# TensorE instead of DMAs spreads the fourth head pair in steps 0 to 3 of a linear-attention and feed-forward kernel

## The chip, the cores and the metric

The kernel runs on one core of one Trainium2 chip. The metric is the device time of one execution, in microseconds (us).

## The reference

Two stages. The first is a recurrent attention over 768 tokens, for 4 sequences and 8 heads of 48 channels; the second a feed-forward block over all 3072 tokens (384 channels, 2048 hidden), with no expert routing in it.

```python
for t in range(S):                       # r, k, v: (4, 8, 768, 48); w, u: (8, 48)
    cur   = u * k_t (outer) v_t
    y[t]  = r_t @ (state + cur)
    state = w * state + k_t (outer) v_t
x = y.transpose(0, 2, 1, 3).reshape(3072, 384)
h = x @ w_in
g = h * tanh(log1p(exp(h)))
out = g @ w_out
```

## The kernel before

**Attention.** The 768 tokens are cut into 6 chunks of 128 tokens; with 4 sequences this makes 24 steps, s = 4 * chunk + sequence. A step holds r and k of its chunk transposed (tile `rk`; for steps 2 and 3 `rkx`), k in natural layout (`kn`, later `rkn`) and v (`v`, for steps 2 and 3 `vx`). VectorE scales r and k by powers of w (L381). In steps 0 to 3 the diagonal terms come from a product `q` (L392, VectorE), eight columns by TensorE (`sd`, L399) and a copy (L402, ScalarE); ScalarE then writes the diagonal matrices of the 8 heads into `P` (L426). TensorE forms the scores `pa` (L456), VectorE puts those below the diagonal into `P` under a mask (L463, one instruction for each of two halves), and TensorE multiplies `P` by v into `yt` (L487). From step 4 on the product with the running state `S` is added (L495). `st` (L524) is the outer product of k and v that advances the state; for it VectorE first multiplies k by a table (`kn<-kn,TKn`, L440).

**Rows of x.** The feed-forward contracts over 384 channels in 3 blocks of 128 rows. Heads go in pairs; a pair fills rows 0 to 47 and 64 to 111 of a block. Rows 48 to 63 and 112 to 127 of the three blocks take the fourth pair, 16 channels each. In `finish`, ScalarE copies the fourth pair from `yt` to a side tile `st` (L568), then the first three pairs to `x` (L573), and six DMAs on SyncE's queue move the side tile's rows to their places in `x` (L585). In steps 0 to 3 these six DMAs come for every step, later for every two steps. Event `x{s}` says that x of step s is complete.

**Feed-forward.** Tokens of one chunk of all four sequences make a group g (512 columns). A group has 16 up tiles n (128 hidden channels each, tile `hp`, then copied to `hb` at L748) and 16 down tiles (`acc`). Between them ScalarE runs sigmoid, arctangent and sine with two table loads (L643 to L649) and VectorE a product (L654 in group 0). In group 0 the matmuls are fp32 (L632 up, L676 down); from group 1 on three fp32r products take their place (L610). The first four up tiles of group 0 are cut into pieces of one sequence, 3 matmuls each (L707, 16 pieces), so that they can start when `x0` is complete. Up tile 4 is the first whole one. Down tile n - 6 follows up tile n.

**Weights.** 16 chunks of 768 KB are loaded by GpSimd's queue (`wraw`, L268), 8 for `w_in` and 8 for `w_out`, and converted from 64-bit to 32-bit floats by ScalarE (L286, L292) and VectorE (L288 to L298; the last of a conversion is L298). I write U0, U1, ... for the chunks of `w_in` (two up tiles each) and D0, D1, ... for those of `w_out`. Later each chunk is split into two fp32r halves (L311 ScalarE, L313 VectorE).

**Order.** The kernel writes out the order of every engine's instructions itself. Small generators (threads) yield an engine and a cost or the name of an event; a planner (`Flow`) picks the thread that can go first, ties by rank. A planned wait of TensorE longer than `WARM_MIN` is filled with dummy matmuls (`idle`, L229) by `flow.fill`, until the first piece of L707 is issued. The lead constants shift ranks, in up tiles: `L_IN` and `L_OUT` for the conversions and splits of `w_in` and `w_out`, `L_ATT` for the attention steps. On the chip each engine runs its list in order and waits at each instruction for what it needs; so an instruction that waits holds up all that stand behind it on that engine. SyncE's queue holds the loads of `rk`, `kn`, `rkn`, `v` and the DMAs of L585.

Of the kernel before, what the change touches and what calls it, by code (L numbers as in the profile page):

```python
# [10 lines left out]
F32 = mybir.dt.float32  # L11
F32R = mybir.dt.float32r
# [5 lines left out]
ALU = mybir.AluOpType  # L18
# [3 lines left out]
B, H, S, D = 4, 8, 768, 48  # L22
NP = H // 2
C = 128
NC = S // C
NS = NC * B
DM, DFF = H * D, 2048
KT = DM // 128
# [12 lines left out]
HALVES = (slice(0, 64), slice(64, 128))  # L41
# [9 lines left out]
LAG = 6  # L51
LO0, HI0, LO1, HI1 = 0.10, 0.92, 0.05, 0.85
LAT, LAT0 = 0.15, 0.13
WARM0, WARM_MIN, FILL = 32, 0.3, 1.1
DMA_LAT = 2.0

COST = dict(dve=1.5)
FREE = dict(pe=8.0, act=4.5, dve=2.0, pool=1.7, sp=1.0)

L_ATT, L_V, L_IN, L_OUT, L_GATE, L_EVAC, L_PUT, L_FIN = 4, -2, 2, 4, 2, 12, 9, 4  # L60


class Flow:
# [60 lines left out]
def dve(cols, fast=False):  # L124
    return {"dve": 0.14 + cols / (1900 if fast else 950)}


def act(cols):
    return {"act": 0.1 + cols / 1060}


def pe(us):
    return {"pe": us}
# [3 lines left out]
def rwkv_mish_kernel(ctx, tc, rkT, rkN, vN, wT, w_in, w_out, consts, rkF, vF, wF, uF, outT):  # L137
    nc = tc.nc
# [4 lines left out]
    work = main.enter_context(tc.tile_pool(name="work", bufs=2))  # L143
# [10 lines left out]
    us = cst[:, 256 : 256 + 2 * NP].rearrange("d (p q) -> d p q", q=2)  # L154
# [15 lines left out]
    loaded = {}  # L170
# [10 lines left out]
    def prologue():  # L181
# [16 lines left out]
        nc.vector.tensor_copy(TRK[:, 1], TR[:, :, ::-1])  # L198
        flow.set("TRK")

    def token_table():
        dw = work.tile([128, NP, 2, D], F32, name="dw", tag="fa", bufs=1)
        yield {"pool": 1.5}
        nc.gpsimd.memset(dw, 0.0)
        yield "TRK"
        for par in range(2):
            r = ROWS[par]
            yield dve(192)
            nc.vector.tensor_tensor(
                out=dw[r, :, par], in0=ident[r, r].unsqueeze(1).broadcast_to([D, NP, D]),  # L210
                in1=w128[r].unsqueeze(2).broadcast_to([D, NP, D]), op=ALU.mult,
            )
        yield pe(1.0)
        t = ps.tile([128, 512], F32, name="tkn", tag="acc1")
        for p in range(NP):
            nc.tensor.matmul(
                t[:, 2 * p * D : 2 * (p + 1) * D], lhsT=TRK[:112, 1, p, :],
                rhs=dw[:112, p].rearrange("d q e -> d (q e)"), start=True, stop=True,
            )
        yield act(384)  # L220
        nc.scalar.copy(out=TKn, in_=t[:, :DM])
        flow.set("TKn")
# [3 lines left out]
    def keep_warm(n):  # L226

        for _ in range(n):
            nc.tensor.matmul(idle[:, :256], lhsT=zeros, rhs=zeros.unsqueeze(1).broadcast_to([128, 2, 128]), start=True, stop=True)  # L229
# [3 lines left out]
    flow = Flow(FREE)  # L233
    flow.events["wt"] = 3.5
    for c in range(2 * NW):
        flow.events[f"raw{c}"] = 8.5 + 4.0 * min(c, 3) + 2.3 * max(c - 3, 0)
    flow.fill = lambda us: keep_warm(int(us * FILL / 0.112))
    ok = const.tile([32, 1], I32, name="ok")

    def check_range():  # L240
# [77 lines left out]
    xs, sides = {}, [None]  # L318
# [3 lines left out]
    def load_early():  # L322

        both = work.tile([128, 2, 2, NP, C], F32, name="rkx", tag="x")
        vx = work.tile([128, 2, 2, NP, 64], F32, name="vx", tag="gh")
        for s in range(B):
            if s < 2:
                rk = stage.tile([128, 2, NP, C], F32, name="rk", tag="rk")
                v = stage.tile([128, 2, NP, 64], F32, name="v", tag="v")
            else:  # L330
                rk, v = both[:, s - 2], vx[:, s - 2]
            if s % 2 == 0:
                kn = stage.tile([128, 2, DM], F32, name="kn", tag="rkn")
            loaded[s] = rk, kn[:, s % 2], v
            yield {"sp": 2.4}
            nc.sync.dma_start(rk[:112], rkT[s])
            flow.set(f"rk{s}")
            yield {"sp": 1.4}
            nc.sync.dma_start(v, vN[s])
            flow.set(f"v{s}")  # L340
        yield "x0"
        for s in range(B):
            yield {"sp": 0.55}
            nc.sync.dma_start(loaded[s][1], rkN[s][:, 1])
            flow.set(f"rkn{s}")

# [122 lines left out]
    def outputs(s):  # L469
        c, b = divmod(s, B)  # L470
        last = c == NC - 1
        yield f"masked{s}"
        yield f"v{s}"
        if c:
            yield f"state{s - B}"
            if not last:
                yield f"keys{s}"
        if s:
            yield f"y{s - 1}"
        yield from paced(s, 1)  # L480
        yield pe(1.05 * (1 + (c > 0)) + (0.6 if 0 < c < NC - 1 else 0))
        rk, n, v = loaded[s][:3]
        P = Ps.pop(s)
        y = ps.tile([128, 512], F32, name="yt", tag="yt")
        for p in range(NP):
            for par in range(2):
                nc.tensor.matmul(  # L487
                    y[HALVES[par], p * C : (p + 1) * C], lhsT=v[:, par, p, :], rhs=P[:, p, par, :],
                    start=not c or p == 0, stop=not c,
                )  # L490
        if c:
            for p in range(NP):
                for par in range(2):
                    r = ROWS[par]
                    nc.tensor.matmul(  # L495
                        y[r, p * C : (p + 1) * C], lhsT=Sc[b][r, p, :], rhs=rk[r, 0, p, :], start=False, stop=p == NP - 1
                    )
        flow.set(f"out{s}")
        flow.start(finish(s, y), rank(s) - L_FIN)
        if not c:  # L500
            flow.start(first_state(s), s - 899.5)
        elif not last:
            st = state_products(s, "pa0")
            r = slice(0, 112)
            yield dve(192)
            nc.vector.tensor_tensor(
                out=Sc[b][r], in0=Sc[b][r], in1=w128[r].unsqueeze(2).broadcast_to([112, NP, D]), op=ALU.mult
            )
            for par in range(2):
                r = ROWS[par]  # L510
                yield dve(192)
                nc.vector.tensor_tensor(
                    out=Sc[b][r], in0=Sc[b][r], in1=st[r, : NP * D].rearrange("d (p e) -> d p e", p=NP), op=ALU.add
                )
        if c:
            flow.set(f"state{s}")
# [28 lines left out]
    def finish(s, y):  # L545
        g, b = divmod(s, B)
        if b == 0:
            if g >= 2:
                yield f"ups{g - 2}"
            if g:  # L550
                xs[g] = work.tile([128, KT, B, 2, C], F32R, name="x", tag="x")
            else:
                xs[g] = work.tile([128, KT, B, 1, C], F32, name="x0", tag="x")
        x = xs[g]
        y = y.rearrange("m (k t) -> m k t", k=NP)
        if g:
            if b % 2 == 0:
                yield f"x{s - 1}"
                sides[0] = work.tile([128, 2, 2, C], F32R, name="st3", tag="st3", bufs=1)
            side = sides[0][:, b % 2]  # L560
        else:
            if b % 2 == 0 and b:
                yield f"x{s - 1}"
            if b % 2 == 0:
                sides[0] = work.tile([128, 2, 1, C], F32, name="st0", tag="st3", bufs=1)
            side = sides[0][:, b % 2]
        yield act(128)
        nc.scalar.copy(out=side[:, 0], in_=y[:, 3])  # L568
        if g:
            yield dve(128)  # L570
            nc.vector.tensor_tensor(out=side[:, 1], in0=y[:, 3], in1=side[:, 0].bitcast(F32), op=ALU.subtract)
        yield act(384)
        nc.scalar.copy(out=x[:, :, b, 0], in_=y[:, :3])  # L573
        if g:
            yield dve(384)
            nc.vector.tensor_tensor(out=x[:, :, b, 1], in0=y[:, :3], in1=x[:, :, b, 0].bitcast(F32), op=ALU.subtract)
        flow.set(f"y{s}")
        if g and b % 2 == 0:
            return
        n = 2 if g else 1  # L580
        yield {"sp": 0.6}
        for k in range(KT):
            for par in range(2):
                o = 64 * par
                nc.sync.dma_start(  # L585
                    x[o + D : o + 64, k, b + 1 - n : b + 1].bitcast(F32).rearrange("e b a t -> e (b a t)"),
                    sides[0][o + 16 * k : o + 16 * k + 16, b % 2 + 1 - n : b % 2 + 1].bitcast(F32).rearrange("e b a t -> e (b a t)"),
                )
        if n == 2:
            flow.set(f"x{s - 1}")  # L590
        flow.set(f"x{s}")

    def place(s, piece):
# [239 lines left out]
    for c in range(len(W_ORDER)):  # L833
        i, f = W_ORDER[c]
# [12 lines left out]
    with tc.If(in_range < 128 * NP):  # L847
# [3 lines left out]
        with tc.tile_pool(name="any1", bufs=1) as work:  # L851
# [22 lines left out]
            with tc.For_i(0, S, TB) as t0:  # L874
# [6 lines left out]
                for t in range(TB):  # L881
# [7 lines left out]
                    for hf in range(2):  # L889
                        y = ps.tile([128, 512], F32, name="hp", tag="hp", bufs=2)  # L890
# [5 lines left out]
        with tc.tile_pool(name="any2", bufs=1) as work:  # L896
            xt = work.tile([128, KT, 2, 64], F32, name="xt")
            x = work.tile([128, KT, 1, 2, C], F32R, name="x")
            for b in range(B):
                with tc.For_i(0, S, 128) as t0:  # L900
# [4 lines left out]
                    t = ps.tile([128, 512], F32, name="t", tag="yt")  # L905
# [4 lines left out]
                    t = t[:, : KT * 128].rearrange("m (k t) -> m k t", k=KT)  # L910
# [79 lines left out]
```

## Time and profile before

| | us |
|---|---|
| median of 3 runs | 568.77 (568.34 to 572.46) |
| the profiled execution | 566.41 |
| its span, first to last instruction | 563.8 |
| TensorE busy (dummy matmuls included) | 535.8 |
| VectorE busy | 372.9 |
| ScalarE busy | 401.7 |
| granted TensorE clock, mean | 0.96 |

The profile is of one execution. Busy times are sums over the span. A row of the timeline gives start, duration, engine, line, operation, tiles, count, and in square brackets how long the engine had stood idle before it and what ended that. The profile counts two matmuls and two weight loads for one fp32 matmul of the program.

### The profile page before, as it was taken

The numbers are of one execution on the slowest core, as the hardware profiler recorded it, in microseconds if no ns is written. First come the engines' busy times: TensorE is split into PE (matmuls) and PEld (weight loads), VectorE is DVE, ScalarE is ACT, GpSimd is POOL, SyncE is SP. The second block draws the span as 40 slices with busy tenths as digits, with TensorE's granted clock in tenths as the row PEclk, the third lists the DMA queues.
The fourth block names the chain that finished last, engine by engine and source line by source line (L and its number), as shares of the span: only waits on it lengthen the run. The fifth ranks groups of instructions, "written<-read, shape, count | busy, mean of one in ns | idle before, by whom it ended". The sixth has DMA issues, their size and how long they took to land. (4 is left out here: it accounts for less than half of the span.)

```text
span 563.8 us, 8124 instructions
## 1 busy us (share of the span) xinstructions
PE 535.8 (95%) x3223; PEld 406.5 (72%) x3223; DVE 372.9 (66%) x560; ACT 401.7 (71%) x479; POOL 10.6 (2%) x26
## 2 busy tenths in 40 slices
PE   6996986999999999999999999999999999999995
PEld 5875743454566787877878887788887778888884
DVE  5554798799677788557587667685666664455552
ACT  2642699577788778887866867865958785859770
POOL 4110000000000000000000000000000000000000
PEclk8758888899999999999999999999999999999998
DMA  8993522120302430302422122322024000010001
GB/s 286 352 405 148 163 68 73 34 80 1 94 1 80 132 98 9 86 5 94 131 80 65 29 59 67 104 80 77 18 80 128 24 0 16 0 51 6 1 0 60
DMA packets 17902, 46.36 MB, mean 82 GB/s; under 512 B 3200, under 2 KB 4096, under 8 KB 17856
## 3 DMA queue, kind: packets, MB, share of 16 engines
q1 hardware_dynamic: 12816, 28.13, 17.2%
q0 software_dynamic: 2304, 12.58, 5.9%
q10 hardware_dynamic: 2736, 5.05, 2.5%
q8 instruction: 27, 0.44, 0.3%
q14 instruction: 19, 0.16, 0.1%
HBM read 38.87 MB, written 4.72 MB: 77 GB/s over the span
## 5 line engine op out<-in xcount | busy, mean ns | idle before, releaser
L610 PE MATMUL hp<-x,w 128*128 128x512 f32 x720 | 182.3, 397 | 0.0
L610 PE MATMUL acc<-gh,w 128*128 128x512 f32 x480 | 159.8, 389 | 0.0
L610 PEld LDWEIGHTS hp<-x,w 128*128 128x128 f32 x720 | 132.7, 188 | 31.6 <-issue 2.6
L610 PEld LDWEIGHTS acc<-gh,w 128*128 128x128 f32 x480 | 90.1, 188 | 18.8
L610 PE MATMUL acc<-gl,w 128*128 128x512 f32 x240 | 93.4, 389 | 0.0
L643 ACT ACT_TABLE_LOAD x48 | 61.6, 1283 | 15.8 <-DVE gf L654 8.0
L748 DVE COPY hb<-hp 128x512 f32<-128x512 f32 x49 | 33.8, 690 | 52.2 <-PE hp L610 46.0
L643 ACT ACTIVATE fa<-hb,bias_ln 128x1024 f32<-128x1024 f32 x48 | 55.3, 1151 | 13.2 <-DVE hb L656 12.7
L656 DVE TENSOR_TENSOR hb<-hb,fa 128x1024 f32<-128x1024 f32 x40 | 48.8, 1220 | 21.4 <-ACT fa L649 21.4
L649 ACT ACT_TABLE_LOAD x48 | 61.6, 1283 | 0.9
L610 PEld LDWEIGHTS acc<-gl,w 128*128 128x128 f32 x240 | 45.0, 188 | 9.4
L646 ACT ACTIVATE fa<-fa 128x1024 f32<-128x1024 f32 x48 | 50.9, 1060 | 1.1
L649 ACT ACTIVATE fa<-fa 128x1024 f32<-128x1024 f32 x48 | 50.9, 1060 | 0.5
L664 DVE TENSOR_TENSOR gl<-hb,gh 128x1024 fp32r<-128x1024 f32 x40 | 48.8, 1220 | 2.1 <-ACT gh L660 1.8
L463 DVE COPY_PREDICATED P<-cst,pa 128x512 f32<-128x512 uint32 x48 | 34.4, 730 | 17.5 <-PE pa L456 17.4
L748 ACT COPY hb<-hp 128x512 f32<-128x512 f32 x47 | 27.5, 585 | 25.3 <-PE hp L610 16.5
L676 PE MATMUL acc<-gf,wraw 128*128 128x512 f32 x96 | 44.6, 600 | 0.0
L632 PE MATMUL hp<-x,wraw 128*128 128x512 f32 x72 | 35.5, 633 | 6.8 <-DVE wraw L298 6.8
L381 DVE TENSOR_TENSOR rk<-rk,TRK 112x512 f32<-112x512 f32 x44 | 29.7, 684 | 5.2 <-DMA rk<-in_rkT_dram 5.2
L676 PEld LDWEIGHTS acc<-gf,wraw 128*128 128x128 f32 x96 | 18.8, 198 | 19.7 <-issue 19.0
L660 ACT CAST gh<-hb 128x1024 fp32r<-128x1024 f32 x16 | 16.8, 1052 | 21.0 <-DVE hb L656 13.2
L632 PEld LDWEIGHTS hp<-x,wraw 128*128 128x128 f32 x72 | 14.3, 207 | 22.1 <-issue 14.6
(86 smaller groups left out, 540.3 us busy)
## 6 DMA issues: line engine op xcount, KB each, us to landing
rk<-in_rkT_dram SPq DMA_DIRECT2D x22, 448.0 KB, 4.2
rkn<-in_rkN_dram SPq DMA_DIRECT2D x20, 384.0 KB, 4.3
wraw<-in_w_in_dram POOLq DMA_DIRECT2D x8, 768.0 KB, 19.2
wraw<-in_w_out_dram POOLq DMA_DIRECT2D x8, 768.0 KB, 19.6
v<-in_vN_dram SPq DMA_DIRECT2D x22, 256.0 KB, 4.3
out_dram<-ob ACTq DMA_DIRECT2D x18, 256.0 KB, 2.0
x<-st SPq DMA_DIRECT2D x60, 32.0 KB, 2.0
rkx<-in_rkT_dram SPq DMA_DIRECT2D x2, 448.0 KB, 18.4
```

Of the source, the lines that this page charges most:

```text
L381: nc.vector.tensor_tensor(out=rk[:112, a], in0=rk[:112, a], in1=TRK[:112, a], op=ALU.mult)
L463: nc.vector.copy_predicated(out=Ps[s][:, :, par], mask=mask.unsqueeze(1).broadcast_to([128, NP, C]), data=pa[par].rearrange("j (p i) -> j ...
L610: nc.tensor.matmul(out, lhsT=a, rhs=m, start=first and n == 0, stop=last and n == 2)
L632: nc.tensor.matmul(hp[:, :T], lhsT=e[:, fs], rhs=o.x[:, k, :, 0], start=k == 0, stop=k == KT - 1)
L643: nc.scalar.activation(o.g, o.hb, AF.Sigmoid, bias=bias_ln2, scale=1.0)
L646: nc.scalar.activation(o.g, o.g, AF.Arctan)
L649: nc.scalar.activation(o.g, o.g, AF.Sin, scale=2.0)
L656: nc.vector.tensor_tensor(out=o.hb, in0=o.hb, in1=o.g, op=ALU.mult)
L660: (nc.scalar.copy if engine == "act" else nc.vector.tensor_copy)(out=o.gh, in_=o.hb)
L664: nc.vector.tensor_tensor(out=o.gl, in0=o.hb, in1=o.gh.bitcast(F32), op=ALU.subtract)
L676: nc.tensor.matmul(a, lhsT=whole[1, f // WG][:, ws], rhs=o.gf[:, j], start=f == 0, stop=f == NF - 1)
L748: (nc.scalar.copy if engine == "act" else nc.vector.tensor_copy)(out=o.hb[:, j], in_=h)
```

## The change

For steps 0 to 3 `finish` no longer copies the fourth pair to a side tile and issues no DMA. Instead ScalarE copies the fourth pair's v, 16 channels for each of three blocks, to the last 16 of 64 columns of a zeroed tile (`pre` for even steps, `pre2` for odd ones; 48 columns stay zero), and TensorE adds a second product to each block of `yt` in the same accumulation: `P` of the fourth pair by that tile. So `yt` has the rows of `x` in their places, 6 matmuls by v and 6 by the spread tile where there were 8, and one ScalarE copy writes `x`. GpSimd zeroes both tiles ahead of its first weight load. The loads of `kn` for steps 0 to 3 no longer wait in the planner for `x0`. Dummy matmuls: 28 at the start for 32; later gaps filled from 0.5 us on, with at most 16. `L_IN` 2 to 6, `L_OUT` 4 to 8, `L_ATT` 4 to 3.

```diff
-WARM0, WARM_MIN, FILL = 32, 0.3, 1.1
+WARM0, WARM_MIN, FILL = 28, 0.5, 0.7
-L_ATT, L_V, L_IN, L_OUT, L_GATE, L_EVAC, L_PUT, L_FIN = 4, -2, 2, 4, 2, 12, 9, 4
+L_ATT, L_V, L_IN, L_OUT, L_GATE, L_EVAC, L_PUT, L_FIN = 3, -2, 6, 8, 2, 12, 9, 4
...
+    pre = work.tile([128, 2, 2, KT, 64], F32, name="pre", tag="fa", bufs=1)
+    pre2 = work.tile([128, 2, KT, 64], F32, name="pre2", tag="st3", bufs=1)
+    nc.gpsimd.memset(pre, 0.0)
+    nc.gpsimd.memset(pre2, 0.0)
+    dw = pre[:, 0].rearrange("d a b c -> d (a b c)").rearrange("d (p q e) -> d p q e", p=NP, q=2)
+    spread = (pre[:, 1], pre2)
...
-    flow.fill = lambda us: keep_warm(int(us * FILL / 0.112))
+    flow.fill = lambda us: keep_warm(min(16, int(us * FILL / 0.15)))
...
-        yield "x0"
         for s in range(B):
-            yield {"sp": 0.55}
+            yield {"sp": 1.0}
             nc.sync.dma_start(loaded[s][1], rkN[s][:, 1])
...
+        else:
+            if s >= 2:
+                yield f"out{s - 2}"
+            engine = yield {**act(96), "dve": 0.25}
+            v = loaded[s][2]
+            (nc.scalar.copy if engine == "act" else nc.vector.tensor_copy)(
+                out=spread[s % 2][:, :, :, D:], in_=v[:, :, KT, :D].rearrange("t q (k e) -> t q k e", k=KT)
+            )
...
-        for p in range(NP):
+        for p in range(NP if c else KT):
             for par in range(2):
-                nc.tensor.matmul(
-                    y[HALVES[par], p * C : (p + 1) * C], lhsT=v[:, par, p, :], rhs=P[:, p, par, :],
-                    start=not c or p == 0, stop=not c,
-                )
+                out = y[HALVES[par], p * C : (p + 1) * C]
+                nc.tensor.matmul(out, lhsT=v[:, par, p, :], rhs=P[:, p, par, :], start=not c or p == 0, stop=False)
+                if not c:
+                    nc.tensor.matmul(
+                        out, lhsT=spread[s % 2][:, par, p, :], rhs=P[:, KT, par, :], start=False, stop=True
+                    )
...
+        if not g:
+            yield act(384)
+            nc.scalar.copy(out=x[:, :, b, 0], in_=y[:, :KT])
+            flow.set(f"y{s}")
+            flow.set(f"x{s}")
+            return
...
-        yield {"sp": 0.6}
+        yield {"sp": 3.6}
```

How the order moves, at three places. On SyncE's queue, after the loads of `rk` and `v` of steps 0 to 3, before the change:

```order
L339 DMA vx<-in_vN_dram 128x512
L585 DMA x_305<-st_306 16x128 x6
L344 DMA kn<-in_rkN_dram 128x384 x4
L585 DMA x_305<-st_306 16x128 x6
L585 DMA x_305<-st_448 16x128 x12
L352 DMA rk<-in_rkT_dram 112x1024
```

and with it (the load of `vx` is the same instruction, four lines further down in the file):

```order
L343 DMA vx<-in_vN_dram 128x512
L347 DMA kn<-in_rkN_dram 128x384 x4
L355 DMA rk<-in_rkT_dram 112x1024
L360 DMA rkn<-in_rkN_dram 128x768
L355 DMA rk<-in_rkT_dram 112x1024
```

All 24 small DMAs are gone, and the loads of `kn` and of steps 4 and 5 stand directly behind `vx`.

On TensorE, around `y` of step 1 and the first piece of an up tile (`hp<-x`), before:

```order
L229 MATMUL idle<-zeros 128x256
L399 MATMUL sd<-cst,q 128x2 x4
L487 MATMUL yt<-P,v 64x128 x8
L707 MATMUL hp<-x_305,wraw 128x128 x3
L456 MATMUL pa_393<-rkx 128x128
```

and with the change (`pre` is the spread tile of step 0, `pre_98` that of step 1, whose matmuls go on behind the last row):

```order
L501 MATMUL yt<-P,pre 64x128
L402 MATMUL sd<-cst,q 128x2 x4
L715 MATMUL hp<-x_310,wraw 128x128 x3
L499 MATMUL yt<-P,v 64x128
L501 MATMUL yt<-P,pre_98 64x128
```

The first piece stands ahead of `y` of step 1 instead of behind it, and the dummies between are gone.

On VectorE, around the two masks of step 3 (`pa_453` and `pa_454` before, `pa_427` and `pa_428` with the change), where `kn<-kn,TKn` waits for the loads of `kn`, `we` and `wraw` are conversions of weights, and L313 or L317 a split. Before:

```order
L440 TENSOR_TENSOR kn<-kn,TKn 128x384 x4
L294 TENSOR_SCALAR we<-we 128x768
L463 COPY_PREDICATED P<-cst,pa_453 128x4x128
L296 SCALAR_TENSOR_TENSOR we<-wraw,we 128x768
L463 COPY_PREDICATED P<-cst,pa_454 128x4x128
L298 ISA wraw<-wraw,we 128x768x2
L290 TENSOR_SCALAR we<-we 128x768
L313 TENSOR_TENSOR w<-wraw,w 128x768
```

and with the change:

```order
L443 TENSOR_TENSOR kn<-kn,TKn 128x384 x2
L294 TENSOR_SCALAR we<-we 128x768 x2
L466 COPY_PREDICATED P<-cst,pa_427 128x4x128
L298 TENSOR_SCALAR we<-we 128x768
L466 COPY_PREDICATED P<-cst,pa_428 128x4x128
L300 SCALAR_TENSOR_TENSOR we<-wraw,we 128x768
L298 TENSOR_SCALAR we<-we 128x768
L302 ISA wraw<-wraw,we 128x768x2
L300 SCALAR_TENSOR_TENSOR we<-wraw,we 128x768
L317 TENSOR_TENSOR w<-wraw,w 128x768
L294 TENSOR_SCALAR we<-we 128x768
L302 ISA wraw<-wraw,we 128x768x2
```

The masks still stand behind all waits for `kn`. Chunks U2 and U3 are now converted side by side right there, and further on, between the end of D0's conversion and the end of U7's, VectorE's list has 98 instructions where it had 109.

More of the change, by code (lines that the diff above doesn't have):

```diff
@@ L199, in prologue @@
         flow.set("TRK")
+    pre = work.tile([128, 2, 2, KT, 64], F32, name="pre", tag="fa", bufs=1)
[4 more added lines that the diff above has]
+    spread = (pre[:, 1], pre2)
     def token_table():
-        dw = work.tile([128, NP, 2, D], F32, name="dw", tag="fa", bufs=1)
-        yield {"pool": 1.5}
-        nc.gpsimd.memset(dw, 0.0)
         yield "TRK"
@@ L473, in outputs @@
         yield f"v{s}"
+        if s:
+            yield f"y{s - 1}"
         if c:
@@ L477, in outputs @@
                 yield f"keys{s}"
-        if s:
-            yield f"y{s - 1}"
+        else:
[6 more added lines that the diff above has]
+            )
         yield from paced(s, 1)
-        yield pe(1.05 * (1 + (c > 0)) + (0.6 if 0 < c < NC - 1 else 0))
+        yield pe(1.05 * (1 + (c > 0)) + (0.6 if 0 < c < NC - 1 else 0) if c else 1.5)
         rk, n, v = loaded[s][:3]
@@ L555, in finish @@
         y = y.rearrange("m (k t) -> m k t", k=NP)
[L556 to L566, printed above, removed]
+        if not g:
[4 more added lines that the diff above has]
+            return
+        if b % 2 == 0:
+            yield f"x{s - 1}"
+            sides[0] = work.tile([128, 2, 2, C], F32R, name="st3", tag="st3", bufs=1)
+        side = sides[0][:, b % 2]
         yield act(128)
         nc.scalar.copy(out=side[:, 0], in_=y[:, 3])
-        if g:
-            yield dve(128)
-            nc.vector.tensor_tensor(out=side[:, 1], in0=y[:, 3], in1=side[:, 0].bitcast(F32), op=ALU.subtract)
+        yield dve(128)
+        nc.vector.tensor_tensor(out=side[:, 1], in0=y[:, 3], in1=side[:, 0].bitcast(F32), op=ALU.subtract)
         yield act(384)
         nc.scalar.copy(out=x[:, :, b, 0], in_=y[:, :3])
-        if g:
-            yield dve(384)
-            nc.vector.tensor_tensor(out=x[:, :, b, 1], in0=y[:, :3], in1=x[:, :, b, 0].bitcast(F32), op=ALU.subtract)
+        yield dve(384)
+        nc.vector.tensor_tensor(out=x[:, :, b, 1], in0=y[:, :3], in1=x[:, :, b, 0].bitcast(F32), op=ALU.subtract)
         flow.set(f"y{s}")
-        if g and b % 2 == 0:
+        if b % 2 == 0:
             return
-        n = 2 if g else 1
-        yield {"sp": 0.6}
+        yield {"sp": 3.6}
         for k in range(KT):
@@ L585, in finish @@
                 nc.sync.dma_start(
-                    x[o + D : o + 64, k, b + 1 - n : b + 1].bitcast(F32).rearrange("e b a t -> e (b a t)"),
-                    sides[0][o + 16 * k : o + 16 * k + 16, b % 2 + 1 - n : b % 2 + 1].bitcast(F32).rearrange("e b a t -> e (b a t)"),
-                )
-        if n == 2:
-            flow.set(f"x{s - 1}")
+                    x[o + D : o + 64, k, b - 1 : b + 1].bitcast(F32).rearrange("e b a t -> e (b a t)"),
+                    sides[0][o + 16 * k : o + 16 * k + 16].bitcast(F32).rearrange("e b a t -> e (b a t)"),
+                )
+        flow.set(f"x{s - 1}")
         flow.set(f"x{s}")
```

## The prediction

> **What bounds the kernel now.** The page's busy shares and its slices come first.
>
> ```profile
> span 563.8 us, 8124 instructions
> PE 535.8 (95%) x3223; PEld 406.5 (72%) x3223; DVE 372.9 (66%) x560; ACT 401.7 (71%) x479; POOL 10.6 (2%) x26
> PE   6996986999999999999999999999999999999995
> ```
>
> TensorE is the bound on average, but its row has holes in the first seven slices of 14.1 us only. So I split the span with the windows view (core, then busy time and count of PE, PEld, DVE, ACT and POOL, granted clock, DMA share, GB/s).
>
> ```profile
> 26.00:66.00 40.00, 31.71 (x249) 27.34 (x250) 22.16 (x36) 15.18 (x37) 2.22 (x5) 0.74 0.67 253
> 66.00:141.10 75.10, 66.66 (x366) 34.92 (x366) 66.66 (x113) 60.74 (x85) 0.00 (x0) 0.93 0.21 59
> 141.10:557.00 415.90, 415.90 (x2465) 327.09 (x2460) 270.95 (x378) 312.94 (x329) 0.00 (x0) 1.00 0.18 55
> ```
>
> From 141.1 us to 557.0 TensorE is never idle, at full clock, with the other engines at 65% to 75%. Its work there does not change. So the question is **how much earlier TensorE reaches the point that is at 141.1 now**, the start of up tile 14. Ahead of it lie a head (to 65.85, the first whole up tile) and a middle. The timeline of TensorE shows where each loses time.
>
> ```profile
> 45.79 0.47 PE L707 MATMUL hp<-x,wraw 128*128 128x128 f32 x2 [2.88 <-DMA x<-st]
> 56.19 2.39 PE L707 MATMUL hp<-x,wraw 128*128 128x128 f32 x18
> 65.85 2.85 PE L632 MATMUL hp<-x,wraw 128*128 128x512 f32 x6
> 98.29 4.88 PE L632 MATMUL hp<-x,wraw 128*128 128x512 f32 x6 [4.99 <-DVE wraw L298]
> 128.09 2.85 PE L632 MATMUL hp<-x,wraw 128*128 128x512 f32 x6 [1.77 <-DVE wraw L298]
> 141.12 2.85 PE L632 MATMUL hp<-x,wraw 128*128 128x512 f32 x6
> ```
>
> In the head it waits for rows of x that DMAs bring; in the middle for conversions (L298), and after the long wait of 4.99 us its first tile takes 4.88 us instead of 2.85.
>
> **The head, removed.** Who waits for the small DMAs, in the timelines of ScalarE and SyncE's queue:
>
> ```profile
> 47.75 0.27 ACT L568 COPY st<-yt 128x128 f32<-128x128 f32 x1 [12.17 <-DMA x<-st]
> 47.91 0.49 ACT L573 COPY x<-yt 128x384 f32<-128x384 f32 x1
> 29.01 2.19 SPq L344 DMA_DIRECT2D kn<-in_rkN_dram x4
> 32.88 27.16 SPq L585 DMA_DIRECT2D x<-st  x18
> ```
>
> The side tile has one buffer, so step 2's copy waited 12.17 us until step 1's six DMAs had landed, behind four loads of `kn`. `y` of step 3 could follow only then, and 18 DMAs kept the queue to 60 us. All of that goes. What is late next? VectorE's list:
>
> ```profile
> 25.99 0.69 DVE L392 TENSOR_TENSOR q<-rkx 112x512 f32<-112x512 f32 x1 [5.91 <-PE idle L229]
> 44.69 0.56 DVE L440 TENSOR_TENSOR kn<-kn,TKn 128x384 f32<-128x384 f32 x1 [3.36 <-DMA kn<-in_rkN_dram]
> 47.11 0.72 DVE L463 COPY_PREDICATED P<-cst,pa 128x512 f32<-128x512 uint32 x1
> 57.55 0.96 DVE L296 SCALAR_TENSOR_TENSOR we<-wraw,we 128x768 uint32<-128x768 uint32 x1
> 58.42 0.55 DVE L294 TENSOR_SCALAR we<-we 128x768 uint32<-128x768 uint32 x1
> 58.89 0.95 DVE L298 CUSTOM_DVE_ANT_0 wraw<-wraw,we 128x1536 uint16<-128x1536 uint16 x1
> ```
>
> The `q` at 25.99 is that of step 3. The dummies named had ended before, so it waited for its load of `rkx`, which the change leaves where it is; shorter filling ahead of this point gains nothing, since the masks of step 1 stand behind that `q`. The second bound is the last `kn`: the masks of step 3 stand behind it in both lists, and it came at 44.69. With the change its load follows `vx` on the queue:
>
> ```profile
> 5.46 0.59 SPq L339 DMA_DIRECT2D vx<-in_vN_dram  x1
> DMA to landing us min/median/max: 19.0/21.0/23.0
> DMA to landing us min/median/max: 6.9/9.6/13.8
> ```
>
> The second row is `vx`, the third `kn`. The last `vx` lands at 5.46 + 23.0 = 28.5. Behind it the four `kn`, 768 KB, come at the latest after what they needed before, 44.7 - 29.0 = 15.7 us: 44.2, hardly a gain. At the earliest they come soon after 28.5, but TensorE's own list is the next bound then, priced by these rows:
>
> ```profile
> 24.69 1.05 PE L399 MATMUL sd<-cst,q 112*128 112x2 f32 x8
> 53.77 1.09 PE L487 MATMUL yt<-P,vx 128*64 128x128 f32 x16
> 58.50 0.56 PE L524 MATMUL st<-vx,kn 128*48 128x48 f32 x16
> 36.36 4.21 PE L707 MATMUL hp<-x,wraw 128*128 128x128 f32 x18
> 125.16 1.16 PE L456 MATMUL pa<-rk 48*128 48x128 f32 x16
> 28.00:42.00 14.00, 12.64 (x77) 0.54 1.03 405
> ```
>
> Steps 0 to 3 have 12 matmuls for 8, so 24 records for 16: a `y` takes 1.09 x 24/16 = 1.64 us, 0.55 more than before. A piece has 6 records at 2.39/18 = 0.133: 0.8. Step 1's masks end at 25.99 + 2.4 = 28.4. From there to `y` of step 3 TensorE's list holds two `y`, one `sd`, two scores, six pieces and two `st`: 3.3 + 1.05 + 2.3 + 4.8 + 1.1 = 12.5 us, to 40.9 at full clock. At the 0.54 of the window from 28 to 42 it would be 23.1 us, to 51.5. So the masks of step 3 bind if `kn` comes after 37.7. I take **41.0** for `kn`, the middle of 37.7 and 44.2. From there the `kn` instruction, three conversions and two masks, with spacings of 0.47 and 0.61 us, end 3.2 us later, as the chain from 44.69 to 47.83 did: 44.2, which a clock at half for the first 7 of those us (28.4 + 7 + 9 = 44.4) would give as well.
>
> Then `y` of step 3 ends at 45.8, and ScalarE's one copy adds 0.7 (0.49 and the handover). Nine pieces stand behind it in the new order: 7.2. Two `st` add 1.1. **The first whole up tile starts at 54.8** instead of 65.85. The ends are 51.5 (`y` of step 3 at 40.9) and 62.1 (at 51.5); with `kn` at 44.2 alone it is 58.0.
>
> Those ends hang on the clock, which shorter filling could lower:
>
> ```profile
> 42.00:48.00 6.00, 2.19 (x22) 0.99 0.89 348
> 48.00:51.00 3.00, 3.00 (x27) 0.50 0.08 27
> ```
>
> A third of 6 us busy, and the clock falls to half only behind it, though the next 3 us are full of work. [...]
>
> [...]
>
> **The middle.** TensorE's own work from up tile 4 to up tile 14, by the spacings of these rows:
>
> ```profile
> 112.13 1.09 PE L487 MATMUL yt<-P,v 128*64 128x128 f32 x16
> 114.66 2.85 PE L632 MATMUL hp<-x,wraw 128*128 128x512 f32 x6
> 117.34 2.74 PE L676 MATMUL acc<-gf,wraw 128*128 128x512 f32 x6
> 119.92 2.74 PE L632 MATMUL hp<-x,wraw 128*128 128x512 f32 x6
> ```
>
> 10 up and 8 down tiles at 2.62 (2.68 and 2.58 from row to row), four times scores (1.09) and `y`, `S` and `st` together (114.66 - 112.13 = 2.53): 47.2 + 4.4 + 10.1 = 61.7 us. It took 141.1 - 65.85 = 75.3, so 13.6 are lost. With nothing lost tile 14 would start at 54.8 + 61.7 = 116.5. But it needs chunk U7, and VectorE converts. Its list has 109 instructions from the end of D0's conversion to the end of U7's; the window counts one more at its edge.
>
> ```profile
> 65.13 0.95 DVE L298 CUSTOM_DVE_ANT_0 wraw<-wraw,we 128x1536 uint16<-128x1536 uint16 x1
> 66.08:138.65 72.57, 64.15 (x110) 0.93 0.21 61
> 137.74 0.94 DVE L298 CUSTOM_DVE_ANT_0 wraw<-wraw,we 128x1536 uint16<-128x1536 uint16 x1
> ```
>
> VectorE was 88% busy there, and a step of its list took 72.57/110 = 0.66 us, waits in. With the leads raised the same stretch has 98 instructions, since splits and later steps fall behind it: 64.7 us. It begins at the end of D0's conversion. Behind the masks (44.2) stand 14 instructions up to it, by the spacings of the three conversions quoted eight of 0.87 and five of 0.47, and a copy of 0.3, 9.6 us, and a wait that I put at 1.4, since the second split among them needs room that tile 1's last piece frees: 55.2. So U7 is ready at **55.2 + 64.7 = 119.9**, 3.4 us after TensorE could take it. I add 0.6 for matmuls at a low clock behind such waits: tile 14 at 120.5, **20.6 us earlier**. Behind it the list holds the splits that were pushed back. Group 1, with three products for one, leaves more time for each chunk, so I take no more than another 0.6 us off.
>
> ```profile
> 66.08:138.65 72.57, 58.62 (x82) 0.93 0.21 61
> 2.23 0.42 POOL L204 MEMSET dw<- 128x384 f32 x1
> ```
>
> ScalarE (first row) works 58.6 of those 72.6 us, so it is less tight. GpSimd zeroes three times the columns of the second row, 1.3 us, ahead of the first weight load; the load at 25.99 hides that, and without this cover the head would be later by as much. Each spread copy is a ScalarE instruction of 96 columns, a quarter of the 0.49 us copy and a fixed part, while ScalarE waits 12.17 us in one place there.
>
> **The sum.** The profiled execution took 566.4 us (span 563.8 and 2.6 around it), below the three timed runs, whose median is 568.77. 20.6 - 0.6 = 20.0: 546.4 for the profile, and **548.8** against the median.
>
> **The rivals.**
> (a) TensorE never waits in the middle: 116.5, or 113.2 with the early head, so 24.6 to 27.9 us earlier: 541 to 544. For it: 98 instructions at 64.15/110 = 0.58 are 57.2 us, and 55.2 + 57.2 = 112.4. Against it: VectorE would have to have no wait at all. 15%.
> (b) Only the head is gained and the middle loses its 13.6 us again, since conversions, masks and copies share one list: 11.0 us, 557.8; with the late `kn` 7.9 us, 560.9. For it: VectorE is 88% busy. Against it: 11 instructions fewer ahead of U7. 25%.
> (c) Slower: each conversion now stands ahead of something that TensorE waits for. VectorE's list is in order, so a mask or copy of `hp` in the middle can stand behind one whole conversion, 0.87 + 0.87 + 0.47 + 0.47 = 2.7 us. With 4 steps and 10 up tiles waiting so, 38 us come on top of 20.0 gained: 587. It decides from 20.0/14 = 1.4 us each. Against it: of the 13.6 us lost in the middle now, 4.99 + 1.77 are the two waits for L298 and 2.0 the slow tile, so at most 4.8, 0.3 each, are for masks and copies. 4%.
> (d) The change does not do what it says: the small DMAs are gone, but TensorE's list at 0.54 of its clock is as late as they were. Tile 4 at 62.1, and the middle loses its 13.6 us again: 3.8 us gained, 565. For it: the window from 28 to 42. Against it: that list has fewer gaps. Within 1%: 6%.
> The forecast itself, 14 to 24.6 us, has 50%.
>
> About 1% (5.7 us) is what a measurement here can tell from no change. Faster by more has 0.90, within it 0.06, slower 0.04. The range from 541 to 561 takes in (a) and (b) with the bounds of `kn`; it leaves out (c) and (d).
>
> **What the profile after would show.** No wait for small DMAs ahead of the early pieces; the last `kn` at 38 to 44 and `y` of step 3 some 3 us behind it; the first whole up tile at 51 to 59; waits for L302 ahead of tiles 8, 10 or 14 of 1 to 4 us; tile 14 at 116 to 124; then no idle time to the end. I am wrong if the first whole tile comes at 62 or later, if the clock stays at half between 30 and 55, if waits for masks in the middle exceed 6 us together, or if TensorE waits in group 1 for the splits that moved back.

## The result and the profile after

The changed kernel takes 544.16 us (median of four runs, 542.85 to 547.55) where the kernel before takes 568.56 (567.73 to 572.46). The ratio is 0.957, with a 95% interval from 0.951 to 0.963. Forecast were 548.8 us and a range from 541 to 561. The profiled execution took 543.95 us, its span is 542.1. One execution of the kernel with only the leads raised, below, took 606.72 us at a mean granted clock of 0.834, a slow state, and is left out of that kernel's figures.

The page after, busy shares and TensorE's slices (13.6 us each):

```profile
span 542.1 us, 8094 instructions
PE 519.7 (96%) x3230; PEld 395.5 (73%) x3230; DVE 377.0 (70%) x565; ACT 397.7 (73%) x467; POOL 10.7 (2%) x27
PE   5899999979999999999999999999999999999993
```

Behind the first two slices one hole is left of those before (the 7, around 113 us). The windows view gives the stages: head, a piece of it, middle, rest.

```profile
26.00:50.50 24.50, 22.46 (x268) 20.43 (x267) 20.48 (x33) 16.43 (x36) 2.76 (x6) 1.00 1.03 357
28.00:42.00 14.00, 12.37 (x158) 11.12 (x155) 10.31 (x19) 7.17 (x19) 2.23 (x5) 1.00 1.03 345
50.50:117.40 66.90, 63.33 (x370) 33.13 (x366) 61.21 (x102) 63.10 (x83) 0.00 (x0) 1.00 0.29 97
117.40:533.40 416.00, 416.00 (x2466) 327.08 (x2460) 280.76 (x393) 304.45 (x317) 0.00 (x0) 1.00 0.18 55
```

In the same 14 us from 28 to 42 TensorE now runs 158 records at full clock instead of 77 at 0.54. From 117.4 on it is never idle, as before from 141.1. VectorE's list of the head and TensorE's timeline say what releases what:

```profile
24.61 0.69 DVE L395 TENSOR_TENSOR q<-rkx 112x512 f32<-112x512 f32 x1 [3.37 <-DMA rkx<-in_rkT_dram]
37.91 0.56 DVE L443 TENSOR_TENSOR kn<-kn,TKn 128x384 f32<-128x384 f32 x1 [2.91 <-DMA kn<-in_rkN_dram]
40.52 0.72 DVE L466 COPY_PREDICATED P<-cst,pa 128x512 f32<-128x512 uint32 x1
50.51 0.96 DVE L302 CUSTOM_DVE_ANT_0 wraw<-wraw,we 128x1536 uint16<-128x1536 uint16 x1
```

```profile
41.29 0.45 PE L499 MATMUL yt<-P,vx 128*64 128x128 f32 x4 [0.40 <-DVE P L466]
42.74 3.80 PE L715 MATMUL hp<-x,wraw 128*128 128x128 f32 x30
50.48 2.85 PE L640 MATMUL hp<-x,wraw 128*128 128x512 f32 x6
72.07 2.85 PE L640 MATMUL hp<-x,wraw 128*128 128x512 f32 x6 [0.38 <-DVE wraw L302]
113.45 0.43 PE L499 MATMUL yt<-P,v 128*64 128x128 f32 x2 [2.14 <-DVE P L466]
114.92 1.09 PE L499 MATMUL yt<-P,v 128*64 128x128 f32 x14 [1.04 <-DVE P L466]
117.44 2.85 PE L640 MATMUL hp<-x,wraw 128*128 128x512 f32 x6
122.70 2.74 PE L640 MATMUL hp<-x,wraw 128*128 128x512 f32 x6
```

No row of the head waits for a small DMA any more. The last `kn` is late next, then the masks of step 3 and `y` of step 3. The first whole up tile starts at 50.48 instead of 65.85: **15.4 us** from the head. Tile 14 starts at 117.44 instead of 141.12, 23.7 us earlier, so the middle gives **8.3 us** more. In the middle one wait for a conversion is left (0.38); the other waits are in step 7, 2.14 and 1.04 us for masks.

Behind tile 14 TensorE's work takes the same 416 us, but the span is only 21.7 us shorter. The rest is in the tail, in the last copy to the output buffer:

```profile
558.68 0.58 ACT L683 COPY ob<-acc 128x512 f32<-128x512 f32 x1 [2.36 <-SPq L847]
537.17 0.59 ACT L691 COPY ob<-acc 128x512 f32<-128x512 f32 x1 [4.48 <-SPq L855]
```

It stood idle 2.36 us before (first row) and 4.48 after. The same row has 2.38 in a second profile of the changed kernel, so that differs from execution to execution and need not come from the change.

For the experiments I use up tile 15 as the mark: from it to TensorE's end the kernels before and after and the first four below take 410.7 to 411.2 us. In the kernel before its row is

```profile
146.38 2.74 PE L632 MATMUL hp<-x,wraw 128*128 128x512 f32 x6
```

From tile 4 to tile 15 TensorE's own work would be 61.7 (the prediction's sum) + 5.26 (117.44 to 122.70) = 67.0 us. The profile says 68.7: it took 72.22 us, of which it stood idle for 3.57.

### The profile page after: what moved, and what is told of

Same layout as the page of the kernel before. It is cut to its first block, busy times and chain, and to the rows that moved or that the text cites. A ratio compares the mean times of both kernels' runs of the same rounds, so it can differ in the third digit from the quotient of the medians.

```text
span 542.1 us, 8094 instructions
## 1 busy us (share of the span) xinstructions
PE 519.7 (96%) x3230; PEld 395.5 (73%) x3230; DVE 377.0 (70%) x565; ACT 397.7 (73%) x467; POOL 10.7 (2%) x27
## 3 DMA queue, kind: packets, MB, share of 16 engines
q0 software_dynamic: 2304, 12.58, 6.7%
## 5 line engine op out<-in xcount | busy, mean ns | idle before, releaser
L756 DVE COPY hb<-hp 128x512 f32<-128x512 f32 x55 | 38.0, 690 | 53.4 <-PE hp L618 51.1
L756 ACT COPY hb<-hp 128x512 f32<-128x512 f32 x41 | 24.1, 587 | 31.8 <-PE hp L618 23.6
L640 PE MATMUL hp<-x,wraw 128*128 128x512 f32 x72 | 33.8, 605 | 0.4 <-DVE wraw L302 0.4
L499 PEld LDWEIGHTS yt<-P,v 128*64 128x64 f32 x344 | 19.0, 136 | 13.8 <-DVE P L466 6.4
## 6 DMA issues: line engine op xcount, KB each, us to landing
wraw<-in_w_out_dram POOLq DMA_DIRECT2D x8, 768.0 KB, 23.6
```

The source lines that it names most:

```text
L499: nc.tensor.matmul(out, lhsT=v[:, par, p, :], rhs=P[:, p, par, :], start=not c or p == 0, stop=False)
L640: nc.tensor.matmul(hp[:, :T], lhsT=e[:, fs], rhs=o.x[:, k, :, 0], start=k == 0, stop=k == KT - 1)
L756: (nc.scalar.copy if engine == "act" else nc.vector.tensor_copy)(out=o.hb[:, j], in_=h)
```

## The experiments

The kernel before, beside the first four: 567.33 us (564.47 to 568.11). Each of these four changes one part.

**The old filling in the changed kernel.**

```diff
-WARM0, WARM_MIN, FILL = 28, 0.5, 0.7
+WARM0, WARM_MIN, FILL = 32, 0.3, 1.1
...
-    flow.fill = lambda us: keep_warm(min(16, int(us * FILL / 0.15)))
+    flow.fill = lambda us: keep_warm(int(us * FILL / 0.112))
```

> The changed kernel with the dummy filling of before (32 dummies at the start, 32 instead of 15 ahead of the scores of step 1); nothing else differs. Prediction's theory: shorter filling gains nothing, because the masks of step 1 stand behind the q of step 3, which waits for a load (24.61 us): first whole up tile at 50.5 to 51.5, total within 1.5 us of the changed kernel's 544.2. Rival 1 (filling is part of the gain): 17 more dummies at 0.2 us push scores and y of step 1 back and the head keeps all of it: first whole tile at 53 to 54, total 547 to 548. Rival 2 (clock): more filling holds the clock, and the head is earlier by 1 us or more.

Measured 544.32 us (541.59 to 547.12), ratio 0.959 (0.955 to 0.963): the changed kernel's time. Filling is worth nothing that can be measured. In the profile the first whole tile comes later than expected, at 52.55 and not by 51.5, and the rows say why:

```profile
39.98 0.56 DVE L443 TENSOR_TENSOR kn<-kn,TKn 128x384 f32<-128x384 f32 x1 [2.84 <-DMA kn<-in_rkN_dram]
52.55 2.85 PE L640 MATMUL hp<-x,wraw 128*128 128x512 f32 x6
121.56 3.40 PE L640 MATMUL hp<-x,wraw 128*128 128x512 f32 x6
127.38 2.74 PE L640 MATMUL hp<-x,wraw 128*128 128x512 f32 x6
```

The last `kn` came 2.07 us later in this execution, and so did the first whole tile: 12.57 us between them here, 12.57 in the first profile after. This profile alone doesn't show that the filling is free, since TensorE stands idle for only 1.35 us ahead of `y` of step 3: with a `kn` 2 us earlier TensorE's own list, later here by the dummies, would have been the bound. That the filling costs nothing rests on the medians.

**The leads back in the changed kernel.**

```diff
-L_ATT, L_V, L_IN, L_OUT, L_GATE, L_EVAC, L_PUT, L_FIN = 3, -2, 6, 8, 2, 12, 9, 4
+L_ATT, L_V, L_IN, L_OUT, L_GATE, L_EVAC, L_PUT, L_FIN = 4, -2, 2, 4, 2, 12, 9, 4
```

> The changed kernel with L_IN, L_OUT, L_ATT back at 2, 4, 4. Theory (the middle's gain comes from the raised leads): head as in the changed kernel, first whole up tile at 50.5 within 1 us, then the middle loses some 10 to 13 us to waits for the last instruction of conversions (L302) instead of 5.3: tile 14 at 122 to 126, total 549 to 553. Rival (VectorE has free time in the shorter head anyway, the leads do nothing): total within 1.5 us of 544.2.

Measured 552.47 us (550.58 to 553.67), ratio 0.975 (0.971 to 0.979). TensorE's timeline:

```profile
47.96 2.85 PE L640 MATMUL hp<-x,wraw 128*128 128x512 f32 x6
64.89 2.08 PE L459 MATMUL pa<-rk 48*128 48x128 f32 x16 [3.27 <-issue]
68.60 5.49 PE L684 MATMUL acc<-gf,wraw 128*128 128x512 f32 x6 [1.63 <-DVE wraw L302]
84.28 4.55 PE L640 MATMUL hp<-x,wraw 128*128 128x512 f32 x6 [2.19 <-DVE wraw L302]
113.74 2.85 PE L640 MATMUL hp<-x,wraw 128*128 128x512 f32 x6 [1.77 <-DVE wraw L302]
132.04 2.74 PE L640 MATMUL hp<-x,wraw 128*128 128x512 f32 x6
```

The head is earlier even than with the change (47.96), by a `kn` that came at 34.04. Here `kn` binds no longer: the distance is 13.9 us, and TensorE runs from 26 to 50 us without a gap. But the middle takes 84.1 us instead of 72.2. TensorE is idle there for 9.9 us instead of 3.6: the waits for conversions are back, 5.6 us together, 1.05 is for masks, and 3.27 stand ahead of the scores of step 5, for which the profile names no releaser. Behind two of the waits for conversions tiles are slow (5.49 and 4.55 us for 2.74 and 2.85), as at a low clock (4.88 us at 0.57 in the profile before, at 98.29), and TensorE's busy time grows from 68.7 to 74.2 us.

**The leads alone in the kernel before** (the same line, the other way round).

> The kernel before with only L_IN, L_OUT, L_ATT raised to 6, 8, 3. Theory (head and middle are separate terms): head still waits for the small DMAs, first whole up tile at 65 to 66; the middle loses about 6 instead of 13.6 us: total 560 to 563. Rival (conversions can be ahead only where the head leaves VectorE room): no change, 567 to 570.

Measured 556.81 us (556.04 to 557.87 in three runs), ratio 0.983 (0.978 to 0.988), better than the 560 to 563 expected.

```profile
65.21 2.85 PE L632 MATMUL hp<-x,wraw 128*128 128x512 f32 x6
136.83 2.74 PE L632 MATMUL hp<-x,wraw 128*128 128x512 f32 x6
```

The head stays where it was, and the middle falls from 80.5 to 71.6 us. That is 10.5 us in the median, more than I had put on the leads. The rival falls: the gain doesn't need the earlier head.

**All of the change except the removal of the DMAs**: leads and filling as after, `kn` no longer waiting for `x0` in the planner, side tile and six DMAs a step as before.

```diff
...
-        yield "x0"
         for s in range(B):
-            yield {"sp": 0.55}
+            yield {"sp": 1.0}
             nc.sync.dma_start(loaded[s][1], rkN[s][:, 1])
```

> The kernel before with everything of the change but the spreading by TensorE: leads, filling and the loads of kn directly behind vx; the six DMAs of each of steps 0 to 3 stay. Theory (the small DMAs themselves bound the head, through the one side tile): kn is there by 38 us, but step 2's copy still waits for step 1's DMAs and SyncE's queue is held: first whole up tile at 58 to 62, total 553 to 558. Rival (the order of kn ahead of the small DMAs is what matters, the DMAs cost little): first whole tile at 51 to 54, total 544 to 548.

Measured 554.89 us (553.14 to 557.31), ratio 0.979 (0.975 to 0.982). That is 1.9 us below the leads alone, with intervals that overlap, and 10.7 behind the full change.

```profile
40.98 1.51 PE L706 MATMUL hp<-x,wraw 128*128 128x128 f32 x4 [8.37 <-DMA x<-st]
67.60 2.85 PE L631 MATMUL hp<-x,wraw 128*128 128x512 f32 x6
136.19 2.74 PE L631 MATMUL hp<-x,wraw 128*128 128x512 f32 x6
```

Early loads of `kn` alone gain nothing in the head: the first whole tile is as late as before (67.60, and not at 58 to 62 as expected). The place of the wait is another than the theory had. TensorE waits 8.37 us for the first step's small DMAs at 40.98, now that the loads of `kn` stand ahead of them on the queue (before, `kn` stood behind them and the first pieces ran at 30.99), and the copy of step 2 then waits for TensorE. With the small DMAs kept, the head is late in both orders of the queue (65.85 and 67.60). So the head's gain needs the DMAs' removal.

By the start of tile 15, the leads alone are worth 9.6 us (146.38 to 136.83), the rest of the change with the old leads 14.3 (to 132.04), both 23.7 (to 122.70), and 9.6 + 14.3 = 23.9. That this sum fits so well is partly luck: in the profile with the old leads `kn` came early and the head ended 2.5 us before that of the full change. By stages, the middle with the earlier head and the old leads takes 84.1 us, longer than the 80.5 before, so the raised leads take 11.9 us off the middle there and 8.9 off it behind the old head. **The head's gain needs the DMAs gone; the middle's comes from the leads.**

The next kernels ask what binds now. Beside them the kernel before took 566.69 us (564.72 to 568.76).

**The changed kernel once more.**

> The changed kernel as it is, on the same chip as the three edits below. Expected 544.2 us (542 to 547). If the time of the first whole up tile follows the last kn, the distance between the two is again 12.6 us (37.91 to 50.48 in the first profile), wherever the kn lands. The masks of step 7 cost TensorE 3.2 us again.

Measured 544.86 us (543.84 to 549.61), ratio 0.963 (0.960 to 0.967).

```profile
36.66 0.56 DVE L443 TENSOR_TENSOR kn<-kn,TKn 128x384 f32<-128x384 f32 x1 [2.62 <-DMA kn<-in_rkN_dram]
49.24 2.85 PE L640 MATMUL hp<-x,wraw 128*128 128x512 f32 x6
112.19 0.43 PE L499 MATMUL yt<-P,v 128*64 128x128 f32 x2 [2.14 <-DVE P L466]
114.69 1.93 PE L508 MATMUL yt<-rk,S 48*48 48x128 f32 x16
117.35 4.92 PE L640 MATMUL hp<-x,wraw 128*128 128x512 f32 x6
```

Again 12.58 us from `kn` to the first whole tile. Step 7 waits as long as in the first profile, but here the rows behind it are slow, 4.92 us for a tile at a granted clock of 0.56: of this more below.

**`kn` of steps 2 and 3 behind the masks of step 3 on VectorE.**

```diff
     def keys(s):
...
+        if 2 <= s < B:
+            yield "masked3"
```

> In the changed kernel the kn of steps 2 and 3 are put behind the masks of step 3 in VectorE's list. Theory: the last kn bounds y of step 3, so TensorE's 2.0 us of idle time between 26 and 50.5 us go: first whole up tile 10.5 us or less behind the last kn, about 48.7, and 542.4 us in all. Rival: the time of the last kn does not bind, the conversions that now stand behind a waiting kn do (tile 8 waited 0.38 us for one already): the first whole tile comes earlier, up tile 15 at 122.7 as before, 544.

Measured 542.89 us (539.54 to 544.11), ratio 0.958 (0.956 to 0.961), 2.0 us below the changed kernel beside it, with intervals that overlap a little.

```profile
24.05 0.69 DVE L395 TENSOR_TENSOR q<-rkx 112x512 f32<-112x512 f32 x1 [2.26 <-DMA rkx<-in_rkT_dram]
48.06 2.85 PE L642 MATMUL hp<-x,wraw 128*128 128x512 f32 x6
```

The first whole tile comes at 48.06 as the theory had it (48.7), and the middle keeps the gain (tile 15 at 120.26); the rival falls. The head in a single profile also moves with the landing of `rkx`, here early: in the profile of both edits, below, `q` comes at 26.01 and the first whole tile at 50.01. The distance is the better witness: 24.0 us from this `q` in both, where the first three profiles with the distance of 12.6 us from `kn` have 25.5 to 26.5.

**The attention's lead at 4, the other leads as after.**

```diff
-L_ATT, L_V, L_IN, L_OUT, L_GATE, L_EVAC, L_PUT, L_FIN = 3, -2, 6, 8, 2, 12, 9, 4
+L_ATT, L_V, L_IN, L_OUT, L_GATE, L_EVAC, L_PUT, L_FIN = 4, -2, 6, 8, 2, 12, 9, 4
```

> The changed kernel with the lead of the attention's scores at 4 as before the change; the leads of the conversions stay at 6 and 8. Theory: most of what the middle still loses is one place, step 7, whose masks stand behind a gate product that waits for a down tile; with its scores and masks one tile earlier its 3.2 us of waits go: 541.0 us. Rival 1: VectorE's list, 91% busy, is the bound, and the wait only moves to conversions: 544. Rival 2: the lead of 3 is part of what the raised leads gained: 547 or more.

Measured 542.27 us (539.24 to 543.13), ratio 0.955 (0.952 to 0.958): 2.6 us gained. But the waits don't vanish. Step 7 has none now, step 6 has 1.9 us in their place, and its profile shows a low clock behind them, 0.60 from 88 to 92 us:

```profile
91.76 4.75 PE L640 MATMUL hp<-x,wraw 128*128 128x512 f32 x6
```

So, with the 0.38 for a conversion gone too, 1.7 us of waits went, and the median moved by 2.6: the size agrees better with the theory than its mechanism does. Profiles in which the clock fell compare with each other: from tile 4 to tile 15 it is 73.42 us here and 75.45 in the changed kernel beside it, 2.0 less. Rival 1 is half right, since the waits moved, though not to conversions; rival 2 falls, since the lead of 3 was no part of the gain.

**Both edits.**

> Both of these edits in the changed kernel. If both waits are real and apart, 3.2 and 1.8 us add up: 539.2 us. If VectorE's list is the bound, no better than the better of the two, 541 to 544.

Measured 539.75 us (538.82 to 546.53), ratio 0.952 (0.950 to 0.954): 5.1 us below the changed kernel beside it, and the two intervals are apart. Within the noise the two gains add up (2.0 and 2.6).

**Both edits again, and with them the load of `rkx` of step 3 ahead of `vx` of step 2.**

```diff
             nc.sync.dma_start(rk[:112], rkT[s])
             flow.set(f"rk{s}")
-            yield {"sp": 1.4}
-            nc.sync.dma_start(v, vN[s])
-            flow.set(f"v{s}")
+            for w in {0: (0,), 1: (1,), 3: (2, 3)}.get(s, ()):
+                yield {"sp": 1.4}
+                nc.sync.dma_start(loaded[w][2], vN[w])
+                flow.set(f"v{w}")
```

> The kernel with both edits once more, as the measure for the next one. Expected 540 us (538.5 to 542). The first whole up tile follows the q of step 3 by 24.0 us (24.05 to 48.06 and 26.01 to 50.01 in the two profiles with kn behind the masks), no longer the last kn.

> Both edits, and in SyncE's queue the load of rkx of step 3 ahead of the load of vx of step 2 (256 KB). Theory: with kn out of the way the load of rkx is what bounds the head, so its q comes 1 to 1.5 us earlier, and the first whole up tile 24.0 us behind it; 538.7 us, 1.2 under the kernel beside it. Rival: the load is bound by the weights' queue, not by what stands ahead of it on its own; then nothing changes (540), or vx of step 2, later now, holds y of step 2 (541).

Measured 539.40 us (537.91 to 542.93) without and 539.70 (538.39 to 541.46) with the new order of loads; the kernel before took 567.56 there, ratios 0.950 (0.946 to 0.954) and 0.950 (0.946 to 0.953). First without, then with it:

```profile
24.00 0.69 DVE L395 TENSOR_TENSOR q<-rkx 112x512 f32<-112x512 f32 x1 [1.89 <-DMA rkx<-in_rkT_dram]
48.41 2.85 PE L642 MATMUL hp<-x,wraw 128*128 128x512 f32 x6
77.42 2.85 PE L642 MATMUL hp<-x,wraw 128*128 128x512 f32 x6
88.75 2.85 PE L642 MATMUL hp<-x,wraw 128*128 128x512 f32 x6
```

```profile
20.48 1.28 DVE L396 TENSOR_TENSOR q<-rkx 112x512 f32<-112x512 f32 x2
46.82 2.85 PE L643 MATMUL hp<-x,wraw 128*128 128x512 f32 x6
75.84 2.85 PE L643 MATMUL hp<-x,wraw 128*128 128x512 f32 x6
88.55 4.67 PE L643 MATMUL hp<-x,wraw 128*128 128x512 f32 x6
```

The wait for `rkx` is gone and the head ends 1.6 us earlier. But the distance from the second `q` of that row is no longer 24.0 us, it is over 25: TensorE runs from 21.3 to 46.8 without a gap, so its own list is the bound now. Nor is it shown that the new order brought `rkx` earlier, since in the profile with the old leads the two `q` stand together at 20.39 with the old order of loads. In this execution the rows behind step 6's waits are slow again (88.55 - 75.84 = 12.71 us for 11.33, and a tile of 4.67), and more than the 1.6 us was lost again. The medians show no difference, so the theory's 1.2 us were not found.

## Why the prediction came out as it did

Its frame held: TensorE's end moved by what its start of tile 14 moved (23.6 and 23.7 us), and everything behind tile 14 stayed full. Tile 14 was forecast 20.6 us earlier and came 23.7 earlier: the head gave 4.3 us more than the sum had, the middle 1.3 less. By the steps:

- **The small DMAs** as the head's bound: right. Kept beside all the rest, they hold the first whole tile at 67.60.
- **The last `kn`, the step that was most off.** I took 41.0, the middle of 37.7 and 44.2; measured is 37.91. The late end had been read from the 15.7 us that four loads took before. They were issued from 29.0 on, between small DMAs; with the change they are issued from 5.76 on, straight behind `vx`, and the last one is there 10.9 us after the last `vx` (37.91 against 4.64 + 22.4 = 27.0). What made them slow before is not shown by a run of its own. Nor is one profile the whole answer: where VectorE waited for this load, in six profiles of the changed kernel and its variants, it came at 34.04, 36.66, 37.55, 37.91, 39.98 and 41.59, so 41.0 lies within the spread, near its late end.
- **From `kn` to the first whole tile**: 13.8 us forecast, 12.57 and 12.58 measured. The masks came as forecast: 37.91 to 41.24 (40.52 + 0.72) is 3.3 us for 3.2. I had let the pieces wait for ScalarE's copy of step 3 (0.7); the row at 42.74 follows `y` without a gap. And 54 records took 0.125 us each instead of 0.133. So the head gained 15.4 us for 11.1 forecast: 3.1 of the difference from `kn`, 1.2 from this.
- **The clock in the head**, which I feared at half: 1.00 from 28 to 42. So the 23.1 us at 0.54 had no place in it, and rival (d) falls. Why it stood at 0.54 before stays open.
- **Shorter filling gains nothing**: right (544.32 against 544.16). That the change leaves the load of `rkx` where it is holds as far as can be seen: its `q` came at 24.61 for 25.99 before, and at 23.69 and 26.06 in two more profiles.
- **The middle**: the time of VectorE's list was right to 0.5 us, but what waited for it was another instruction. From the end of D0's conversion (51.47, the row at 50.51) I forecast 64.7 us to the end of U7's:

```profile
51.47:115.71 64.24, 60.67 (x332) 31.30 (x331) 58.56 (x99) 60.47 (x79) 0.00 (x0) 1.00 0.28 95
111.41 1.23 DVE L662 TENSOR_TENSOR gf<-hb,fa 128x1024 f32<-128x1024 f32 x1 [0.77 <-PE acc L684]
112.67 0.72 DVE L466 COPY_PREDICATED P<-cst,pa 128x512 f32<-128x512 uint32 x1
114.15 0.72 DVE L466 COPY_PREDICATED P<-cst,pa 128x512 f32<-128x512 uint32 x1
114.76 0.95 DVE L302 CUSTOM_DVE_ANT_0 wraw<-wraw,we 128x1536 uint16<-128x1536 uint16 x1
```

  It is 64.24 us with 99 records for the 98 instructions counted. But TensorE didn't wait for U7 ahead of tile 14. It waited ahead of `y` of step 7, for the masks that stand in the same list just before U7's conversion. Their own predecessor is the gate product at 111.41, which waited 0.77 us for TensorE. So VectorE's list was not the pace by itself. In the second profile with both edits the eighth conversion behind D0's (U7's is the eighth in the changed kernel) ends after 58.89 us and 96 records. I had looked for waits for L302 of 1 to 4 us and found 0.38; the place was wrong. The amount, 4.0 us lost, was near the 5.3 measured (66.96 - 61.7), and this too needs splitting: 3.57 us are idle time, for 3.4 forecast, and the clock stayed at 1.00, so the 0.6 that I had added for a low clock, an estimate, is not in this profile. The other 1.7 are TensorE's own work, 63.4 us where the sum had 61.7, since many rows take a little more than the 2.62 us used for a tile (50.48 to 53.26, for one).
- **The splits pushed back** cost TensorE nothing: 416.00 of 416.00 us busy.
- **Rival (b)**, the middle losing its 13.6 us again, falls: with the leads back it does (84.1 us), with them it doesn't. **Rival (a)** has the measured 544.16 at the edge of its 541 to 544, but not its reason: TensorE did wait 3.6 us in the middle, and the head made up for that. **(c)**: TensorE did wait for masks, 3.2 us together, within the 4.8 us that I had bounded them by.

## What to carry to other kernels

A load's duration shouldn't be carried to another place in the queue: the four `kn` took 9.6 us in the median from issue to landing when issued from 29.0 on, and 24.9 when issued from 5.76 on. When a change moves a load's issue, here by 23 us, price it anew, and from several executions: the last `kn` came between 34.04 and 41.59. Where an engine's in-order list is the pace, forecast the list, but ask for every consumer which instruction of it stands just before the late one: TensorE stood at the masks, 1 us ahead of the conversion that I was watching. A chain is best proved by its link: 12.57 us from the last `kn` to the first whole tile, the same in three profiles with three different landings, showed what bound the head and pointed to the next 2 us. Where the link breaks (13.9 us at a `kn` of 34.04), something else binds, here TensorE's own list.

## What the runs showed of the hardware

The same wait ends at two different clocks. In the first profile of the changed kernel TensorE is granted 1.00 all through step 7's waits of 2.14 and 1.04 us; in the second one the waits are the same to 0.01 us, and behind them:

```profile
111.20:114.60 3.40, 1.36 (x16) 1.04 (x16) 3.37 (x6) 3.34 (x4) 0.00 (x0) 1.00 0.00 0
114.60:117.40 2.80, 2.80 (x35) 2.27 (x33) 2.80 (x6) 2.77 (x4) 0.00 (x0) 0.53 0.00 0
```

TensorE is busy without a gap from 113.67 on, and from 114.6 to 122.1 its granted clock is about half (0.53, then 0.56; the tile at 117.35 takes 4.92 us); tile 15 is 3.2 us further behind tile 13 than in the first profile. Of eight profiles with waits of this kind (3.2 us in step 7 or 1.9 in step 6) the rows behind them are slow in five (tiles of 4.92, 4.75, 4.67 and 3.40 us for 2.85, and in the first profile with both edits a product with `S` of 1.95 for 1.08) and not in three. Why one list gives both outcomes is not shown. The longest gap here is 2.14 us, and the clock stayed low for over 7 us of full work. In the prediction's two rows, from 42 to 51 us before the change, the longest gap is 2.88 us, and the clock is 0.99 up to 48 and 0.50 behind it. What decides whether the clock falls isn't settled by these runs. In these profiles the price of a short wait on TensorE is thus its length plus 0 to 3.2 us, which changes between executions of one list. That may be a good part of the spread of the times of one kernel (543.84 to 549.61), beside the landing of the last `kn`; no run separates the two.
